# A long convolution and a soft mixture of experts: spectra stored and loaded in other shapes, x on other partitions, two loads moved within a step

## The chip, the cores and the metric

The kernel runs on one core of one Trainium2 chip, in float32 throughout. The metric is the device time of one execution in microseconds (us). Before the change it is 912.35 us, the median of three runs (912.24, 912.35 and 916.9 us).

## The reference

Two blocks follow each other. The first is a causal convolution of eight sequences of 5,696 steps and 128 channels with one filter as long as the sequence, by a Fourier transform:

```
Xf = np.fft.rfft(x, n=L, axis=1)        # L = 2 * 5696
Hf = np.fft.rfft(h, n=L, axis=0)
y  = np.fft.irfft(Xf * Hf[None], n=L, axis=1)[:, :S, :]
```

The second takes y as 45,568 tokens of 128 channels. With 8 experts of 4 slots each (32 slots), it mixes tokens into slots, runs the experts and mixes back:

```
logits = x @ phi                                  # (45568, 32)
d = softmax of logits over all tokens;  slot_input = d.T @ x
slot_out[e] = relu(slot_input[e] @ w1[e]) @ w2[e]
c = softmax of logits over the 32 slots;  out = c @ slot_out
```

## The kernel before

**The transform.** A sequence of 5,696 is taken as 89 rows of 64. The transform length is 5,760 = 90 x 64 (`N1`, `N2`). Its first stage runs over the rows and gives 90 frequencies k for each of the 64 columns n. Its second runs over the 64 columns for each k. `g` counts the transformed sequences: g = 0 is the filter `h`, g = 1 to 8 are the eight batches of x. A *chunk* is 4 columns and their 4 mirror columns (`CH = 4`), so a g has 8 chunks (`NJ`), and a *step* t of the main loop handles one chunk in the first stage. Steps 0 to 7 are the filter, 8 to 15 the first batch, and so on to step 71.

**Stage A** (`load_x`, `fold`, `stage_a`). `load_x` brings two chunks at once: 96 rows on partitions 0 to 95 (the filter: 89 rows), for each row 8 near columns and 8 far ones, 4 KB each. `fold` on GpSimd adds and subtracts near and far. `stage_a` multiplies by the table `s1`: its *low* part, each step, gives frequencies below `LOW` = 60 (64 columns of `s1`, 64 partitions for each of two parities `o`); its *high* part, each odd step, gives the other 30 for the two chunks of the last two steps, in four groups of 32 partitions. ScalarE evicts into the tile `fst` (four buffers), and the stores are put on a list `pending` that `flush()` issues later on SyncE's queue (SP). The spectra go to a DRAM tensor `f_g` of shape (90, 64, 2, 128): a low tile in two stores of 60 rows, a high tile in four stores of 30 rows, a row being 4 KB.

**Stage B** (`load_g`, `stage_b1`, `stage_b2`). A *unit* u is 8 frequencies of one g; a g has 12 units (the last has 2 frequencies). `load_g` loads a unit into `gt` (three buffers) as one transfer on 128 partitions, in packets of 1 KB. `stage_b1` does the 64-point transform on TensorE (`bt<-gt,wt`) and multiplies by the filter's spectrum on VectorE. One step later `stage_b2` transforms back (`bz<-yf,vt`), and ScalarE evicts to `zst`, which is stored to `zm` (the first 64 frequencies) or `zr` (the rest). Steps have one and two units in turn; the units of sequence g begin at step 9 + 8g. So unit 0 of a new g is used one step after that g's last chunk has been stored. `prefetch` loads units up to three ahead (`AHEAD = 3`), but those of g only from step 8(g + 1) on.

**Stage C** (`load_main`, `load_rest`, `stage_c1` to `stage_c6`). From step 27 on, each odd step takes a tile T of z, main part (`zc<-zm`) and rest (`zx<-zr`), finishes the inverse transform on TensorE (`bank<-zc,im` at L412, `bank<-zx,ir` at L417), and goes on to logits, softmax and dispatch. The z tiles of step t + 2 are loaded in odd steps; the rest of a batch's first tile, whose data has only just been stored, is loaded in the even step before it is used (t = 26, 34, ... 74).

**Order of the work.** The schedule is written out by hand: each engine executes its instructions in program order. Nearly all transfers are issued by SP in program order, so an SP issue that waits holds all later ones. In the compiled program the transfers carry eight completion counters in turn, and an issue waits until the transfer eight issues before it has landed; so at most eight are in flight.

An even step issues in this order: the first rest of a batch, if it is due; the load of x for step t + 4; the stores of the low spectra; then, around `stage_b1`, the next unit's spectra and the stores of z; then the softmax sums, the dispatch, and the second unit. The main loop ends at step 80, and a tail then finishes the last batch, the experts and the output (stores of `out_dram<-o`).

Of the kernel before, what the change touches and what calls it, by code (L numbers as in the profile page):

```python
# [18 lines left out]
def transform_tables(S, N1, N2, CH, LOW, MAIN, XR):  # L19

    N, R1, HALF, P = N1 * N2, S // N2, N2 // 2, 2 * N2
    k1 = np.arange(N1)  # L30
    alpha = np.pi * (k1 + 0.5) / N1
    m1 = np.arange(R1) - (N1 - 1) / 2
    a1 = np.outer(m1, alpha)
    part = np.stack([np.cos(a1), -np.sin(a1), -np.cos(a1)], 1)
    s1 = np.zeros((P, 2, 3, N2 + HALF))
    for i, r in enumerate((slice(0, R1), slice(XR - R1, XR))):
        s1[r, i, :, 0:LOW] = part[:, :, 0:LOW]
        s1[r, i, :, N2:N2 + N1 - LOW] = part[:, :, LOW:]
# [12 lines left out]
    a2 = m2[None, :, None] * omega[:, None, :]  # L51
    w = np.concatenate([np.cos(a2), np.sin(a2)], 1)
    back = np.arange(N2).reshape(2, HALF).T.reshape(-1)
    NU = (NP + 1) // 2
    turn = (N1 - 1) / 2 * alpha[:, None] + (N2 - 1) / 2 * omega
    wq = np.zeros((2, N2, NP, N2))
    vq = np.zeros((2, N2, NU, 2, N2))
    tn = np.zeros((2, N2, 2, (NU + 1) // 2, 2, 2))
    for a in range(2):
        wq[a] = w[a::2].transpose(1, 0, 2)  # L60
# [10 lines left out]
def kernel(  # L71
# [24 lines left out]
    nc = tc.nc  # L96
# [15 lines left out]
    HP = P // 2  # L112
    NQ = NJ // 2
    assert S == R1 * N2 and R1 == N1 - 1 and D == P and CH == Q == 4
    LOW, MAIN = 60, HP
    XR = -(-R1 // 16) * 16
    ctx.enter_context(tc.manual_schedule())

# [4 lines left out]
    fd = [nc.dram_tensor(f"f_{g}", (N1, N2, 2, D), F32, kind="Internal").ap() for g in range(B + 1)]  # L123
# [54 lines left out]
    def load_x(m, halves=((0, 2 * CH),)):  # L178

        if 2 * m >= (B + 1) * NJ:  # L180
            return
        g, j = divmod(2 * m, NJ)
        if g == 0:
            src, blocks = h, ((0, R1 // 16 * 16), (R1 // 16 * 16, R1))
        else:
            r0 = min((g - 1) * R1, B * R1 - XR) * N2
            src, blocks = x.rearrange("b t d -> (b t) d")[r0:r0 + XR * N2], ((0, XR),)
        src = src.rearrange("(a n) d -> a n d", n=N2)
        t_ = xcs[m % len(xcs)]
        for n0, n in halves:  # L190
            a = (CH * j + n0, N2 - CH * j - n0 - n)
            p = (n0, 2 * CH - n0 - n)
            for r0, r1 in blocks:
                if n == 2 * CH:
                    v = src[r0:r1, a[0]:a[0] + n, :]
                    v = bass.AP(tensor=v.tensor, offset=v.offset,
                                ap=[v.ap[0], [(a[1] - a[0]) * D, 2], [1, n * D]])
                    nc.sync.dma_start(
                        out=t_[r0:r1, :, :, :].rearrange("p s n d -> p s (n d)"), in_=v)
                    continue  # L200
                for s_ in range(2):
                    nc.sync.dma_start(
                        out=t_[r0:r1, s_, p[s_]:p[s_] + n, :].rearrange("p n d -> p (n d)"),
                        in_=src[r0:r1, a[s_]:a[s_] + n, :].rearrange("r n d -> r (n d)"))
        xs[2 * m] = xs[2 * m + 1] = t_

# [16 lines left out]
    def flush():  # L223
        while pending:
            pending.pop(0)()
# [4 lines left out]
    def stage_a(c, high):  # L230

        g, j = divmod(c, NJ)
        st = apool.tile([P, CH, 2, D], F32, name="fst", tag="fst", bufs=4)
        if high:
            groups = [(c_, o, HALF, slice(HP, HP + HALF)) for c_ in (c - 1, c) for o in range(2)]
# [28 lines left out]
    def load_g(u):  # L264
        if u >= (B + 1) * NW:
# [4 lines left out]
        nc.sync.dma_start(  # L270
            out=t_[:, 0:n, :, :].rearrange("p q c d -> p q (c d)"),
            in_=fd[g][8 * w:8 * w + 2 * n].rearrange("(q a) r c d -> (a r) q (c d)", a=2))
        gs[u] = t_

    def stage_b1(u):
# [355 lines left out]
    for t in range(last_front + 1):  # L631
# [58 lines left out]
                softmax_exp(U)  # L690
            flush()
        else:
            if pair(-1) is not None and pair(-1) % NQ == 0:
                load_rest(pair(-1))
            if t < NA:
                load_x(t // 2 + 2)
            flush()
            if t == NJ:
                prefetch(AHEAD - 1)
            slot_b()  # L700
            if W is not None:
                softmax_sum(W)
                dispatch(W)
# [229 lines left out]
```

## Time and profile before

| what | value |
|---|---|
| profiled execution, its own time | 909.23 us |
| its span in the profile | 907.4 us |
| median of the three timed runs | 912.35 us |
| TensorE (PE) busy | 760.2 us, 84% |
| VectorE (DVE) busy | 601.4 us, 66% |
| ScalarE (ACT) busy | 436.8 us, 48% |
| GpSimd (POOL) busy | 399.8 us, 44% |
| SP's transfer queue q1 | 275.74 MB, 89.7% of 16 transfer engines |
| all transfers | 278.33 MB, mean 307 GB/s |

The span is the time from the first to the last instruction that the profiler recorded. The busy shares are means over stages that differ: the filter and the first batches until about 200 us, the full pipeline from there to 640 us, the end of stages B and C to about 830 us, and the output. Which engine or queue ends the wait is read stage by stage. "DMA share" is the time that packets took, summed over the 16 transfer engines of the core and divided by 16 times the stretch; it can go slightly over 1. PEld is TensorE's loading of weights. SPq is SP's sequencer, and the length of one of its DMA entries is the time it took to issue, its own waiting in part included, not the time of the transfer.

### The profile page before, as it was taken

Reading aid. Unit: us, or ns where it says so; the run is one execution under the profiler, and the core shown is the slowest. Engines: PE = TensorE matmul, PEld = TensorE weight load, DVE = VectorE, ACT = ScalarE, POOL = GpSimd, SP = SyncE. Lnnn points to the kernel's source line nnn. Section 1 sums busy time; section 2 is a strip of 40 time slices with the busy share of each in tenths; the row PEclk is TensorE's granted clock in tenths of the full one; section 3 lists DMA queues with packets and bytes.
Section 4 is the critical chain, followed back from the end, with each engine's and each line's share of the span. In section 5 each row is a group of like instructions: output and inputs, shape, how many; then the busy total and the mean of one; then the engine's idle time right before and its main releaser. Section 6 shows DMA issues by size and latency. Waiting matters only on the chain.

```text
span 907.4 us, 21291 instructions
## 1 busy us (share of the span) xinstructions
PE 760.2 (84%) x8308; PEld 387.7 (43%) x8308; DVE 601.4 (66%) x896; ACT 436.8 (48%) x880; POOL 399.8 (44%) x353
## 2 busy tenths in 40 slices
PE   6857778689999989999998999799888877767893
PEld 2212233234444444444444444344444434344793
DVE  2029767568778867886877787678778766653552
ACT  2423234335556545665655655456544444563441
POOL 4634322444555655655655566456332224651000
PEclk9979889999999999999999999899988888766855
DMA  8989999999999999999999999999998768540798
GB/s 267 318 275 343 293 296 337 298 314 376 341 291 375 361 326 308 372 358 299 357 364 335 295 373 348 303 308 346 306 291 304 264 200 341 186 166 1 292 406 335
DMA packets 170443, 278.33 MB, mean 307 GB/s; under 512 B 13543, under 2 KB 128231, under 8 KB 165135
## 3 DMA queue, kind: packets, MB, share of 16 engines
q1 hardware_dynamic: 169336, 275.74, 89.7%
q10 hardware_dynamic: 1008, 1.25, 0.5%
q8 instruction: 66, 1.08, 0.5%
q14 instruction: 33, 0.27, 0.1%
HBM read 147.94 MB, written 129.00 MB: 305 GB/s over the span
## 4 chain that ended last, share of the span: by engine, by line
PE 47%; DMA 23%; ACT 8%; POOL 8%; DVE 6%; issue 6%; SPq 1%; ACTq 0%; DVEq 0%; POOLq 0%
PE bank L241 9%; DMA gt<-f 9%; PE bt L284 9%; PE bz L327 6%; POOL y L430 5%; PE bank L412 4%; DMA f<-fst 4%; PE op L886 3%; PE bank L439 3%; PE bank L417 3%; PE bank L448 2%; DMA zx<-zr 2%; ACT fst L243 2%; DMA out_dram<-o 2%; PE bank L527 2%
## 5 line engine op out<-in xcount | busy, mean ns | idle before, releaser
L241 PE MATMUL bank<-x,s 128*32 128x512 f32 (+1 forms) x1152 | 218.0, 620 | 12.9 <-POOL x L217 8.4
L217 POOL TENSOR_TENSOR x<-xc 128x512 f32<-128x512 f32 x144 | 180.4, 1278 | 107.2 <-PE bank L241 86.5
L284 PE MATMUL bt<-gt,wt 64*64 64x256 f32 x1620 | 125.0, 419 | 72.8 <-DMA gt<-f 33.0
L430 POOL TENSOR_TENSOR y<-y,op 128x512 f32<-128x512 f32 x64 | 77.6, 1213 | 206.8 <-DVE op L404 204.3
L304 DVE TENSOR_TENSOR pi<-bt,Hi 128x1024 f32<-128x1024 f32 x96 | 113.0, 1177 | 83.5 <-PE bt L284 83.3
L243 ACT ACTIVATE fst<-bank 128x512 f32<-128x512 f32 x216 | 122.8, 592 | 86.0 <-PE bank L241 57.7
L332 ACT ACTIVATE zst<-bz 128x1024 f32<-128x1024 f32 x96 | 93.3, 972 | 128.3 <-PE bz L327 109.4
L284 PEld LDWEIGHTS bt<-gt,wt 64*64 64x64 f32 x1620 | 58.3, 141 | 151.2 <-issue 79.1
L312 DVE TENSOR_TENSOR yf<-bt,pi 128x512 f32<-128x512 f32 x192 | 119.4, 663 | 3.3
L304 DVE TENSOR_TENSOR bt<-bt,Hr 128x1024 f32<-128x1024 f32 x96 | 113.0, 1177 | 0.0
L241 PEld LDWEIGHTS bank<-x,s 128*32 128x32 f32 (+1 forms) x1152 | 55.1, 126 | 129.8 <-issue 93.6
L327 PE MATMUL bz<-yf,vt 64*64 64x256 f32 x1440 | 110.4, 404 | 0.0
L327 PEld LDWEIGHTS bz<-yf,vt 64*64 64x64 f32 x1440 | 64.3, 143 | 25.5 <-issue 4.2
L512 POOL TENSOR_TENSOR L<-L,rs 128x512 f32<-128x512 f32 x32 | 33.5, 1048 | 91.6 <-DVE rs L511 66.4
L404 DVE TENSOR_TENSOR y<-bank,y 128x512 f32<-128x512 f32 x32 | 22.1, 692 | 76.7 <-ACT y L420 76.5
L439 PE MATMUL bank<-ident,y 109*128 109x109 f32 x512 | 62.7, 273 | 7.9 <-ACT yt L441 7.9
L504 ACT ACTIVATE L<-L 128x512 f32<-128x512 f32 x32 | 20.2, 630 | 94.7 <-POOL L L501 94.6
L430 POOL TENSOR_TENSOR y<-y,om 128x512 f32<-128x512 f32 x54 | 63.9, 1183 | 2.1
L439 PEld LDWEIGHTS bank<-ident,y 109*128 109x128 f32 x512 | 52.9, 149 | 19.4 <-POOL x L217 14.7
L412 PE MATMUL bank<-zc,im 64*64 64x512 f32 x480 | 60.8, 623 | 0.0
L441 ACT ACTIVATE yt<-bank 128x360 f32<-128x360 f32 x128 | 53.0, 482 | 7.7 <-PE bank L439 7.3
L420 ACT ACTIVATE y<-bank 128x512 f32<-128x512 f32 x32 | 19.1, 596 | 72.6 <-PE bank L417 72.6
(101 smaller groups left out, 862.5 us busy)
## 6 DMA issues: line engine op xcount, KB each, us to landing
gt<-f SPq DMA_DIRECT2D x99, 512.0 KB
f<-fst SPq DMA_DIRECT2D x144, 240.0 KB
zm<-zst SPq DMA_DIRECT2D x128, 256.0 KB
zc<-zm SPq DMA_DIRECT2D x30, 1024.0 KB
xc<-in_x_dram SPq DMA_DIRECT2D x32, 768.0 KB
f<-fst SPq DMA_DIRECT2D x144, 120.0 KB
out_dram<-o SPq DMA_DIRECT2D x16, 1024.0 KB
zx<-zr SPq DMA_DIRECT2D x30, 512.0 KB
```

The lines of the kernel that those rows point to most:

```text
L217: nc.gpsimd.tensor_tensor(out=y_[:, o, :, :], in0=near, in1=far, op=AL.subtract if o else AL.add)
L241: nc.tensor.matmul(p[i * m:(i + 1) * m, :], s1[:, g // B, q + o, cols], columns(c_, o), start=True, stop=True)
L243: nc.scalar.activation(st[:, :, q, :], p[:, :].rearrange("p (n d) -> p n d", d=D), AF.Copy)
L284: nc.tensor.matmul(bt[q * HP:(q + 1) * HP, a, o, :], wt[r, 2 * i + q, :], t_[r, 2 * o + q, :, :].rearrange("p c d -> p (c d)"), start=True ...
L304: nc.vector.tensor_tensor(out=p_, in0=pv, in1=h_, op=AL.mult)
L312: nc.vector.tensor_tensor(out=y_[r, 0:k, c, :], in0=pv[:, :, c, :], in1=pi[r, 0:k, 1 - c, :], op=op_)
L327: nc.tensor.matmul(bz[a * HP:(a + 1) * HP, q, o, :], vt[r, i, a, :], y_[r, a * m + o, :, :].rearrange("p c d -> p (c d)"), start=True, sto ...
L332: nc.scalar.activation(st[:, 0:m, 0:n, :].rearrange("p o q x -> p q o x"), bz[:, 0:n, 0:m, :], AF.Copy)
L412: nc.tensor.matmul(ps[o, c][h_ * HP:(h_ + 1) * HP, :], im[r, c, :], zt[r, h_, :, c, :], start=True, stop=False)
L430: eng.tensor_tensor(out=part_, in0=part(v, 0), in1=o_[:, :, :], op=sign)
L439: nc.tensor.transpose(p[:, i * TR:(i + 1) * TR], ys[T][0:TR, k * CH + i, 0:D], ident[0:TR, 0:TR])
L441: nc.scalar.activation(yt[:, k * CH:(k + 1) * CH, :, :], of_tokens(p), AF.Copy)
```

## The change

Four things change together.

- **Shape of the spectra.** `LOW` becomes 64. The low spectra of a g go to a tensor `fl_g` (parity, 64 frequencies, 32 columns, 2, 128), the high ones to `fh_g` (parity, chunk half, 32, 16 columns, 2, 128), of whose 32 rows 26 are used. Each `fst` tile is now stored whole, in one transfer of 128 rows of 4 KB. A unit of 8 frequencies now lies within one of the two tensors. It is loaded by two transfers (low, one for each parity, onto every second partition) or four (high, onto every fourth). The rows of the table `w` are put in the new order, and in the high part the four matmul groups change their order (parity outside, chunk inside).
- **x on every second partition.** Rows 0 to 63 go to partitions 1, 3, ... 127 and rows 64 to 95 to partitions 32, 34, ... 94, in two transfers in place of one (the filter's rows in three in place of two). The rows of `s1` move along.
- **A new g's first spectra** are loaded at the beginning of step 8(g + 1), ahead of the load of x and the flush, and no longer after that step's first `stage_b1`. There `prefetch` is called with the last unit still in the pipeline plus three, which loads unit 0 (for the filter, units 0 to 2).
- **z's first rest** is loaded after the load of x, after the flush, after the first slot of stage B and another flush.

```diff
-    for i, r in enumerate((slice(0, R1), slice(XR - R1, XR))):
+    spread = np.r_[1:P:2, N2 // 2:N2 // 2 + 2 * (XR - N2):2]
+    for i, r in enumerate((spread[0:R1], spread[XR - R1:])):
...
-    LOW, MAIN = 60, HP
+    LOW, MAIN = HP, HP
...
-    fd = [nc.dram_tensor(f"f_{g}", (N1, N2, 2, D), ...
+    fl = [nc.dram_tensor(f"fl_{g}", (2, LOW, HALF, 2, D), ...
+    fh = [nc.dram_tensor(f"fh_{g}", (2, 2, HALF, HALF // 2, 2, D), ...
...
-            src, blocks = x..., ((0, XR),)
+            src, edges = x..., (0, HP, XR)
...
-            for r0, r1 in blocks:
+            for r0, r1 in zip(edges, edges[1:]):
+                p0 = 2 * r0 - HP - HALF if r0 else 1
+                rows = slice(p0, p0 + 2 * (r1 - r0) - 1, 2)
...
-        k0, k1 = (LOW, N1) if high else (0, LOW)
-        for i, (c_, o, m, _) in enumerate(groups):
-            n0 = o * HALF + CH * (c_ % NJ)
-            pending.append(partial(
-                nc.sync.dma_start,
-                out=fd[g][k0:k1, n0:n0 + CH, :, :].rearrange("k n c d -> k (n c d)"),
-                in_=st[i * m:i * m + k1 - k0, :, :, :].rearrange("k n c d -> k (n c d)")))
+        if high:
+            dst, n0 = fh[g].rearrange("o h k m c d -> (o h k) m (c d)"), CH * (j // 2)
+        else:
+            dst, n0 = fl[g].rearrange("o k n c d -> (o k) n (c d)"), CH * j
+        pending.append(partial(
+            nc.sync.dma_start,
+            out=dst[:, n0:n0 + CH, :].rearrange("p n x -> p (n x)"),
+            in_=st[:, :, :, :].rearrange("p n c d -> p (n c d)")))
...
-        nc.sync.dma_start(
-            out=t_[:, 0:n, :, :].rearrange("p q c d -> p q (c d)"),
-            in_=fd[g][8 * w:8 * w + 2 * n].rearrange("(q a) r c d -> (a r) q (c d)", a=2))
+        if 8 * w < LOW:
+            src = [fl[g][o, 8 * w:8 * w + 2 * n] for o in range(2)]
+        else:
+            k0 = 8 * w - LOW
+            src = [fh[g][o, h_, k0:k0 + 2 * n] for o in range(2) for h_ in range(2)]
+        for i, v in enumerate(src):
+            nc.sync.dma_start(
+                out=t_[i::len(src), 0:n, :, :].rearrange("p q c d -> p q (c d)"),
+                in_=v.rearrange("(q a) r c d -> (a r) q (c d)", a=2))
...
-            if pair(-1) is not None and pair(-1) % NQ == 0:
-                load_rest(pair(-1))
+            if t % NJ == 0:
+                prefetch(wait_b2[-1] + AHEAD if wait_b2 else AHEAD - 1)
             if t < NA:
                 load_x(t // 2 + 2)
             flush()
-            if t == NJ:
-                prefetch(AHEAD - 1)
             slot_b()
+            if pair(-1) is not None and pair(-1) % NQ == 0:
+                flush()
+                load_rest(pair(-1))
```

More of the change, by code (lines that the diff above doesn't have):

```diff
@@ L52, in transform_tables @@
     w = np.concatenate([np.cos(a2), np.sin(a2)], 1)
+    near_low = np.arange(N2).reshape(2, HALF).T.reshape(-1)
+    near_high = np.arange(N2).reshape(2, -1, 2, CH).transpose(1, 3, 0, 2).reshape(-1)
     back = np.arange(N2).reshape(2, HALF).T.reshape(-1)
@@ L59, in transform_tables @@
     for a in range(2):
-        wq[a] = w[a::2].transpose(1, 0, 2)
+        for q in range(NP):
+            wq[a, :, q] = w[2 * q + a][near_low if 2 * q < LOW else near_high]
         for q in range(NP):
@@ L122 @@
                         transform_tables(S, N1, N2, CH, LOW, MAIN, XR))]
-    fd = [nc.dram_tensor(f"f_{g}", (N1, N2, 2, D), F32, kind="Internal").ap() for g in range(B + 1)]
+    fl = [nc.dram_tensor(f"fl_{g}", (2, LOW, HALF, 2, D), F32, kind="Internal").ap() for g in range(B + 1)]
+    fh = [nc.dram_tensor(f"fh_{g}", (2, 2, HALF, HALF // 2, 2, D), F32, kind="Internal").ap()
+          for g in range(B + 1)]
     zm = [nc.dram_tensor(f"zm_{b}", (2, MAIN, HALF, 2, D), F32, kind="Internal").ap() for b in range(B)]
@@ L183, in load_x @@
         if g == 0:
-            src, blocks = h, ((0, R1 // 16 * 16), (R1 // 16 * 16, R1))
+            src, edges = h, (0, HP, R1 // 16 * 16, R1)
         else:
             r0 = min((g - 1) * R1, B * R1 - XR) * N2
-            src, blocks = x.rearrange("b t d -> (b t) d")[r0:r0 + XR * N2], ((0, XR),)
+            src, edges = x.rearrange("b t d -> (b t) d")[r0:r0 + XR * N2], (0, HP, XR)
         src = src.rearrange("(a n) d -> a n d", n=N2)
@@ L198, in load_x @@
                     nc.sync.dma_start(
-                        out=t_[r0:r1, :, :, :].rearrange("p s n d -> p s (n d)"), in_=v)
+                        out=t_[rows, :, :, :].rearrange("p s n d -> p s (n d)"), in_=v)
                     continue
@@ L202, in load_x @@
                     nc.sync.dma_start(
-                        out=t_[r0:r1, s_, p[s_]:p[s_] + n, :].rearrange("p n d -> p (n d)"),
+                        out=t_[rows, s_, p[s_]:p[s_] + n, :].rearrange("p n d -> p (n d)"),
                         in_=src[r0:r1, a[s_]:a[s_] + n, :].rearrange("r n d -> r (n d)"))
@@ L234, in stage_a @@
         if high:
-            groups = [(c_, o, HALF, slice(HP, HP + HALF)) for c_ in (c - 1, c) for o in range(2)]
+            groups = [(c_, o, HALF, slice(HP, HP + HALF)) for o in range(2) for c_ in (c - 1, c)]
         else:
```

## The prediction

> **What bounds the kernel now.** I read the page first, then the busy times by stage, the rates of transfers in fine slices, TensorE's timeline for step lengths, and SP's timeline where a stall begins. The page has no engine that is full: PE 84%, SP's transfer queue 89.7%. By stage (columns: stretch, its length, then busy us and count of PE, PEld, DVE, ACT and POOL, PE's granted clock, DMA share, GB/s) it looks different:
>
> ```profile
> 20.00:50.00 30.00, 22.06 (x102) 6.42 (x98) 0.00 (x0) 11.07 (x20) 17.38 (x14) 0.94 0.96 310
> 57.00:105.00 48.00, 36.71 (x308) 12.40 (x305) 41.28 (x48) 14.33 (x24) 19.83 (x16) 0.93 0.96 309
> 105.00:165.00 60.00, 47.36 (x456) 20.39 (x456) 39.74 (x44) 23.18 (x32) 19.87 (x16) 0.88 0.93 292
> 206.00:640.00 434.00, 407.88 (x4672) 196.15 (x4670) 332.06 (x504) 248.76 (x505) 244.40 (x208) 0.98 1.00 338
> ```
>
> In the full pipeline (206 to 640) PE is busy 94% and the transfer engines 100%, at only 338 GB/s. The output stores at the end run at 406 GB/s. Why so slow in between? Slices of 0.25 us from 406 to 416 (the second line below), beside slices of 0.5 us of the output (the first):
>
> ```profile
> GB/s 418 401 406 410 414 401 406 406 414 406 406 393 414 434 373 385 406 406 406 410 406 410 406 406 401 414 406 406 401 414 410 406 406 406 434 377 393 389 414 410
> ...
> GB/s 371 340 373 332 354 340 279 328 148 131 180 131 246 262 311 262 295 246 262 246 229 217 311 414 397 385 360 311 401 401 365 442 348 340 350 356 356 344 340 348
> ```
>
> From 408 to 411.5 the rate falls to 131-311. SP's timeline (start, us, line, what, number) says what was queued there: x, then two f stores of 60 rows.
>
> ```profile
> 402.43 4.19 SPq L225 DMA_DIRECT2D f<-fst  x4
> 406.74 0.34 SPq L198 DMA_DIRECT2D xc<-in_x_dram  x1
> 407.17 0.88 SPq L225 DMA_DIRECT2D f<-fst  x2
> 408.14 2.52 SPq L270 DMA_DIRECT2D gt<-f  x2
> ```
>
> Behind them comes the new sequence's first unit, and PE waits for it. This happens once in each sequence; the timeline of PE (in brackets the idle time before, and the releaser):
>
> ```profile
> 250.88 1.09 PE L284 MATMUL bt<-gt,wt 64*64 64x256 f32 x16 [0.50 <-DMA gt<-f]
> ...
> 333.89 1.39 PE L284 MATMUL bt<-gt,wt 64*64 64x256 f32 x16 [3.36 <-DMA gt<-f]
> ...
> 416.39 1.95 PE L284 MATMUL bt<-gt,wt 64*64 64x256 f32 x16 [2.07 <-DMA gt<-f]
> ...
> 498.56 1.09 PE L284 MATMUL bt<-gt,wt 64*64 64x256 f32 x16 [1.69 <-DMA gt<-f]
> ...
> 583.22 1.99 PE L284 MATMUL bt<-gt,wt 64*64 64x256 f32 x16 [5.52 <-DMA gt<-f]
> ```
>
> Earlier there are the same waits, longer: 10.23 us at 56.80, 5.16 at 105.16, 3.11 at 172.03. Where no such wait falls, two steps take 20.15 us (low matmuls at 285.82 and 305.97), always the same, so that is compute. From step 29 on, eight steps take 79.78, 83.79, 82.55, 80.83 and 86.18 us (starts 206.04, 285.82, 369.61, 452.16, 532.99, 619.17). With the first one's own 0.50 taken off the floor is 79.3, so the boundary costs 16.7 us over the five sequences, the slow clock after each wait included (16 matmuls in 1.95 us for 1.09).
>
> **The change part by part.**
>
> *Stores of f and loads of x.* Each sequence has 12 f stores for 32, and 6.7% more f bytes (64 + 32 rows for 60 + 30). What a packet takes is in the trace's packet records: from 206 to 639 the 13,234 packets of 4,096 bytes (f, x, zx) have a median of 159 ns and a mean of 194, one in ten near 300, double; the 8,192-byte ones (zc) 309 and 367. All packets sum to 430 us of the 433. At their medians the two sizes would take 29 + 11 us less, and the extra rows 5 more: 395 us, a share of 0.91. Bounds: no relief (435 us with the extra rows) and full relief. I take full relief, because transfers of the new shapes are in this trace already: z's stores of 64 rows from every second partition are two fifths of the 1,024-byte packets, of which nine in ten take 46 ns or less, and the output's 128 rows run at 406 GB/s.
>
> In the pipeline this gives nothing by itself, since PE's 79.3 us per sequence hide it, but it shortens every queue. Where the queue is the bound it counts: in 20-50 the chain of waits is four landings of f in a row (18.91 for 9.80, 29.56 for 5.86, 35.85 for 7.51, 43.79 for 5.44). Packets there show about 5.5 us of excess in those 30, minus 1 for the rows: -4.5 (bounds 0 and -6; PE needs 22 of the 30).
>
> *The filter's loads* are 19 issues for 12, of which two come before the first fold. Eight took 3.71 us, so +0.9 there; the rest waits behind the tables in the queue or adds up to 3. I take +1.
>
> *The split unit loads.* 32 for 12 issues per sequence, and 8 for 4 of x: with f's 12 for 32 SP has 96 issues for 92, at 0.33 to 0.6 us each: +2 us of SP time in 79, hidden by SP's waiting for landings (the waits of SP's f and z issues for earlier transfers are over 100 us). 0; bounds 0 and +2 per sequence. The Trainium skill speaks against it: "DMA: Bandwidth & Descriptors", section "Rules for kernel authors", says two transfers to disjoint partition halves are not worth it and one of 128 partitions should be used, and "Anatomy of one DMA" gives a fixed 2.0 us for each (on another issue path). By that, 180 more unit loads would be up to 360 us one after another; the rows show up to eight in flight and 0.48 us per issue.
>
> *The first unit at the beginning of the step.* It no longer waits for x's issue and two f issues, and three of four high-f issues are gone: 402.43 + about 1 us for the one store is 403.4 for 408.14, 4.7 us earlier, and x (768 KB) and low f (480 KB) are no longer ahead in the queue, 3.7 us at 338 GB/s. Together 8 us earlier against a longest steady wait of 5.52, so these waits go. Of 16.7 us I take -15 (bounds -5 and -17). In exchange x is later by two issues and 512 KB, about 2.5 us; it is used three steps, 30 us, on. The load must find its low stores landed: they were issued in the middle of the step before, and in the pipeline 7 issues lie between.
>
> At the start fewer lie between, and SP stands until the last low store has landed. At 49.24 it did so already (the landing at 49.23 released it). Then the unit took 7.52 us with 1.25 MB ahead, which is 4 us at 310 GB/s: -4 (bounds -1 and -6). For 57-105, VectorE needs eleven filter units at 3.65 us (on the chain one begins at 64.95, the next at 68.64 and 72.23) and a short one of 1.9, 42 us; the first batch's unit came at 48.4, behind loads of 8.14, 6.88 and 7.12 us on the chain. Down to VectorE's floor, with the clock's 0.9: -5 (bounds -2 and -6). At 172.03: -3 (bounds 0 and -3.1). From 105 to 165 the waits of 2.99 us each pair are between PE and VectorE around one `bt` buffer: 0.
>
> *z's first rest.* Six times in the pipeline, and at step 26. It moves past x's two issues, the low store, the unit's loads and two z stores. SP now stands at the z stores until ScalarE's `zst` is done. At step 50: `zst` ends at 427.40, two z issues of 0.4-0.6 us, so zx is issued at about 428.5; before it was 430.01, because SP was late. PE reached L417 at 435.75 without waiting. From 428.5 there are 7.2 us, and when the step comes sooner, `zst` does too, so these 7.2 us stay. Landings of z on the chain took 4.9 to 6.5 us. So late by 0 to 1.5: +0.5 each, +3. At step 26, PE waited 2.28 us; zx goes from 185.22 to about 186.2 and more lies ahead: +1.5 (bounds 0 and +3). In return SP is no longer held by the landing of zr (5.68 us there on the chain). What queues behind the moved load are the step's later stores and the second unit, which is two steps ahead.
>
> *The high part's matmul order*: same count, same forms, 0. After 640: no wait for a unit shows, 0 (bounds -1 and +2).
>
> **The sum:** +1 - 4.5 - 4 - 5 - 3 + 1.5 - 15 + 3 = -26 us. The span 907.4 becomes 881.4, the profiled execution 909.23 becomes 883.2. The median is 3.1 us over that execution, so 912.35 - 26 gives 886. One measurement of this kernel can tell about 0.5% (4.6 us) from no change.
>
> **The rivals.**
>
> *Only the reorder works.* The conflicts between packets stay (x's 32 rows, f's 128). Then the share stays at 1.00 and queues stay long: 435 us of packets against 416 of steps at the floor. The stretch gains nothing beyond what the shorter way of the first unit buys early on: -4, -3 and -3, +4 for late zx, and -5 in the pipeline, about -11: 901. For: nothing here shows x's shape in 4 KB packets. Against: z's stores.
>
> *A wait for zx takes the gt waits' place.* If all eight places ahead hold 256 KB to 768 KB, up to 2.8 MB, a landing takes 8 us, as gt's 8.11: 1-3 us late, seven times, 7 to 21 us, the steady gain gone: between 895 and 910. The trace's four waits of PEld for zx sum to 5.9 us, so there is little slack.
>
> *The end on the other side: the split unit loads run into each other.* 64 or 32 rows per transfer put two transfer engines on the same partitions' ways. If their 1,024-byte packets doubled, as 4 KB ones do here, 30,000 packets at +46 ns over 16 engines are +86 us: 395 + 86 = 481 us for 433, +48, less 8 us of the start: about 952. It decides from +11 ns a packet (21 us, all the slack below 416), and the kernel is slower from about +30 ns. Against: the same shape stores at 46 ns.
>
> **How the numbers follow.** The sum 0.55, with its own range 874 to 895 from the bounds taken together; only the reorder 0.15; late zx 0.15; colliding loads 0.10; a start that loses more than its gain, with the rest near nothing, 0.05. Faster by over 0.5%: 0.55 + 0.14 + 0.09 = 0.78. Within: 0.07. Slower: 0.15, the collisions and part of the start. The range goes from 872, all upper gains, to 912, where the late zx has eaten all; the collisions are left out.
>
> **What would show it.** Right: the DMA share in the full pipeline falls to about 0.92 and no slice stays under 250 GB/s while x and f go; PE's waits for gt at the five boundaries are under 0.5 us and eight steps take 79-80 us; the first b1 comes at 48-50 us and the first batch's at 91-94. Wrong: PE's waits at L417 over 1.5 us each; 1 KB packets above 50 ns or a share of 1.00 with longer steps; SP standing at the first unit of a sequence for over 3 us.

## The result, and the profile after

The changed kernel takes 945.6 us (median of four runs, 943.0 to 946.6) where the kernel before takes 912.3 in the same comparison: 1.036 times as long, 95% interval 1.031 to 1.041. The forecast was 886, with a range that ended at 912. It went to the other side, in part by a rival that had been priced too low.

The busy times by stage of the changed kernel, columns as in the prediction (stretch, its length, busy us and count of PE, PEld, DVE, ACT and POOL, PE's granted clock, DMA share, GB/s):

```profile
8.00:20.00 12.00, 8.76 (x32) 2.25 (x32) 0.00 (x0) 4.76 (x7) 6.16 (x5) 1.00 0.82 249
20.00:50.00 30.00, 25.27 (x112) 7.72 (x112) 0.00 (x0) 12.17 (x22) 20.71 (x18) 0.94 0.99 370
57.00:105.00 48.00, 37.85 (x324) 12.90 (x316) 42.75 (x50) 14.76 (x25) 19.82 (x16) 0.96 0.94 317
206.00:640.00 434.00, 379.20 (x4296) 179.90 (x4294) 305.20 (x465) 228.01 (x464) 225.99 (x193) 0.96 0.94 318
```

The second line holds what was hoped of the wide transfers: 370 GB/s for 310. The last holds the loss. In the full pipeline PE is busy 379 us for 408, and the DMA share has indeed fallen from 1.00 to 0.94, but at 318 GB/s for 338: the transfer engines are not quicker, they now stand idle between transfers. Of the span's 37.2 us more (944.6 for 907.4), 4.6 lie before step 29 (it begins at 210.66 for 206.04), 33.2 in the next five times eight steps (446.3 us for 413.1), and -0.6 behind.

PE's waits for transfers, all in one view (the waits by instruction, operation and releaser: sum in us, count, longest):

```profile
PEld bank L432 <- DMA zx<-zr: 53.5, 7, 11.6
PE bank L432 <- DMA zx<-zr: 47.3, 6, 10.7
PE bt L299 <- DMA gt<-fl: 13.5, 6, 6.0
```

Before, PE had waited 33.0 us for `gt<-f` and 2.5 for zx; now it is 16.7 for gt (the line shown and 3.2 for `gt<-fh`) and 47.3 for zx. The two have changed places, and zx costs more than gt did. PE's timeline shows that it is z's first rest, once in each sequence:

```profile
279.04 1.81 PE L432 MATMUL bank<-zx,ir 26*64 26x512 f32 x16 [4.92 <-DMA zx<-zr]
367.13 2.01 PE L432 MATMUL bank<-zx,ir 26*64 26x512 f32 x16 [7.14 <-DMA zx<-zr]
459.23 2.01 PE L432 MATMUL bank<-zx,ir 26*64 26x512 f32 x16 [10.72 <-DMA zx<-zr]
548.76 2.02 PE L432 MATMUL bank<-zx,ir 26*64 26x512 f32 x16 [8.13 <-DMA zx<-zr]
638.77 2.02 PE L432 MATMUL bank<-zx,ir 26*64 26x512 f32 x16 [8.87 <-DMA zx<-zr]
```

The five waits sum to 39.8 us, against 13.1 us of gt waits in the same stretch before. After each wait the clock is slow for a while: the sixteen matmuls take 2.0 us, elsewhere 1.1, and in the 2.0 us from 459.23 on the granted clock is 0.50. SP's timeline in step 50 (start, us, line, what, number) and, below it, the chain of waits through the longest of them show how zx came to be late:

```profile
444.16 0.53 SPq L233 DMA_DIRECT2D fh<-fst  x1
446.58 1.16 SPq L206 DMA_DIRECT2D xc<-in_x_dram  x2
447.84 1.51 SPq L233 DMA_DIRECT2D fl<-fst  x1
449.45 1.61 SPq L285 DMA_DIRECT2D gt<-fl  x2
451.15 1.27 SPq L233 DMA_DIRECT2D zm<-zst  x2
452.47 0.65 SPq L400 DMA_DIRECT2D zx<-zr  x1
```

```profile
438.65 7.55 DMA zc<-zm
...
452.47 6.71 DMA zx<-zr
459.18 0.04 issue
459.23 2.01 PE bank L432 x16
```

First SP stands until 446.2 for the landing of an earlier zc, because x's issue needs the completion counter of the transfer eight issues before it. Then come seven issues, 5.9 us, and only then zx, which takes 6.7 us to land. Step 50 began at 435.01, so zx is issued 17.5 us into it. Before the change it was issued 7.5 to 9.9 us after the beginning of its step and landed 3.9 to 4.9 us later. In the pipeline that was just in time, between 0.2 us too late and 1.0 us early for PE's matmuls on it. The same step before, SP's timeline and PE's, where zx landed at 434.76:

```profile
430.01 0.35 SPq L385 DMA_DIRECT2D zx<-zr  x1
430.40 0.43 SPq L198 DMA_DIRECT2D xc<-in_x_dram  x1
```

```profile
435.75 1.11 PE L417 MATMUL bank<-zx,ir 26*64 26x512 f32 x16
```

### The profile page after: what moved, and what is told of

Its sections match the earlier page's. It is cut to its first block, busy times and chain, and to the rows that moved or that the text cites. A ratio compares the mean times of both kernels' runs of the same rounds, so it can differ in the third digit from the quotient of the medians.

```text
span 944.6 us, 21328 instructions
## 1 busy us (share of the span) xinstructions
PE 764.5 (81%) x8308; PEld 382.8 (41%) x8308; DVE 601.1 (64%) x896; ACT 437.0 (46%) x880; POOL 399.8 (42%) x353
## 3 DMA queue, kind: packets, MB, share of 16 engines
q10 hardware_dynamic: 1008, 1.25, 0.5%
## 4 chain that ended last, share of the span: by engine, by line
PE 48%; DMA 23%; ACT 8%; issue 6%; POOL 5%; SPq 4%; DVE 4%; DVEq 0%; ACTq 0%; POOLq 0%
PE bank L249 11%; PE bt L299 9%; PE bz L342 7%; DMA zx<-zr 5%; DMA out_dram<-o 4%; PE bank L427 4%; DMA zc<-zm 4%; PE bank L432 4%; PE bank L454 3%; POOL y L445 3%; PE bank L463 2%; ACT fst L251 2%; DMA fl<-fst 2%; ACT zst L347 2%; PE bank L542 2%
## 5 line engine op out<-in xcount | busy, mean ns | idle before, releaser
L249 PE MATMUL bank<-x,s 128*32 128x512 f32 (+1 forms) x1152 | 221.2, 621 | 14.8 <-POOL x L225 11.4
L432 PE MATMUL bank<-zx,ir 26*64 26x512 f32 x480 | 38.9, 707 | 47.3 <-DMA zx<-zr 47.3
L454 PEld LDWEIGHTS bank<-ident,y 109*128 109x128 f32 x512 | 52.5, 148 | 18.1 <-POOL x L225 13.3
```

The source lines that it names most:

```text
L432: nc.tensor.matmul(p[h_ * HP:(h_ + 1) * HP, :], ir[r, :], zx[r, h_, :, :], start=False, stop=True)
L454: nc.tensor.transpose(p[:, i * TR:(i + 1) * TR], ys[T][0:TR, k * CH + i, 0:D], ident[0:TR, 0:TR])
```

## The experiments

Five theories stood at the beginning. P (place): zx's new place alone costs the time. H (handed on): the earlier first unit gains nothing much, because zx becomes the wait. L: more transfers make SP late. Q: whole tiles put more bytes in flight and land later. C: split unit loads collide in the transfer engines. Unless said otherwise the edits stand against the kernel before.

**Each move and the shapes by themselves.** First the changed kernel with only z's first rest back in its old place:

```diff
         else:
+            if pair(-1) is not None and pair(-1) % NQ == 0:
+                load_rest(pair(-1))
             if t % NJ == 0:
...
             slot_b()
-            if pair(-1) is not None and pair(-1) % NQ == 0:
-                flush()
-                load_rest(pair(-1))
```

> The changed kernel with one part undone: z's first rest is loaded at the beginning of the step again, ahead of x. After the change PE stands 47.3 us at the rest's matmuls (six waits of 4.9 to 10.7 us). Theory P (place): zx is late because it was moved past seven issues that took 5.9 us (446.58 to 452.47). Then the six waits fall to under 20 us in sum and the time to 905-922. Theory L (late queue): zx is late because loads of units and x in pieces (40 issues of 0.6 us for 16 of 0.4-0.5 per sequence) make SP late everywhere. Then zx stays late: waits of 30 us or more, time 930 or more. Theory H (handed on): every boundary has one lateness of SP, which PE paid at the unit before and pays at zx once the unit is early; then what is left here is about what the units cost before, 2 to 5 us each, 10-20 us in sum, time 905-915, and part 4 alone shows the same.

926.6 us, 1.013 [1.009, 1.017]. The waits for zx fall from 47.3 to 13.5 us, as P has it, but those for gt rise from 16.7 to 25.3, and the time stays above P's range. The reverse edit, the kernel before with only this load moved:

```diff
-            if pair(-1) is not None and pair(-1) % NQ == 0:
-                load_rest(pair(-1))
             if t < NA:
                 load_x(t // 2 + 2)
             flush()
             slot_b()
+            if pair(-1) is not None and pair(-1) % NQ == 0:
+                flush()
+                load_rest(pair(-1))
```

> The kernel before with one part alone: z's first rest behind x, the stores, the unit's loads and another flush. P: zx goes out some 4 us later than now (430.0 to about 434 at step 50) and lands 5 us on, at 439 against a need at 435.75; 3-4 us late six or seven times, 20-25 us, time 930-937. L: without the pieces SP is not late; under 5 us, time 910-917. H: the unit still stands in the way and gives SP time; 0-10 us, 910-922.

942.8 us, 1.031 [1.026, 1.037]. Its waits, in the same view as above:

```profile
PE bank L417 <- DMA zx<-zr: 35.1, 6, 7.4
PE bt L284 <- DMA gt<-f: 17.6, 7, 9.2
```

P holds: one load moved by a slot, with nothing else changed, costs 28 us, a little more than P expected. In passing it takes nearly all waits for gt out of the pipeline (0.4 us left between 206 and 640), presumably because transfers catch up while PE stands for zx. A step that shows a wait vanish has not shown a gain.

Next the changed kernel with both moves undone, which leaves the shapes:

```diff
-            if t % NJ == 0:
-                prefetch(wait_b2[-1] + AHEAD if wait_b2 else AHEAD - 1)
+            if pair(-1) is not None and pair(-1) % NQ == 0:
+                load_rest(pair(-1))
...
             flush()
+            if t == NJ:
+                prefetch(AHEAD - 1)
             slot_b()
-            if pair(-1) is not None and pair(-1) % NQ == 0:
-                flush()
-                load_rest(pair(-1))
```

> The changed kernel with both moves undone: only the shapes of the spectra's transfers and x's partitions. P: no move, so zx is not late; the shorter queues shorten the units' waits; 895-908. L: zx is late by the pieces alone, 20 us or more of waits at the rest's matmuls, time 920 or more. H: units and zx share the lateness, sum of both waits in the pipeline near the 13 us of the units before, time 903-915.

931.2 us, 1.017 [1.014, 1.021]. The shapes too are a loss. The first-unit waits grow from 13.1 to 29.5 us in the pipeline, although 20 to 50 runs at 375 GB/s. The time is in L's range, but not by L's path: between 206 and 640 PE never waits for zx. Then the earlier first unit alone:

```diff
+            if t % NJ == 0:
+                prefetch(wait_b2[-1] + AHEAD if wait_b2 else AHEAD - 1)
             if t < NA:
                 load_x(t // 2 + 2)
             flush()
-            if t == NJ:
-                prefetch(AHEAD - 1)
             slot_b()
```

> The kernel before with one part alone: a new sequence's first spectra loaded at the beginning of the step. P and L: the units' five waits in the pipeline (13 us, 16.7 with what follows) shrink by more than half, nothing takes their place: 893-902. H: the units' waits go, and zx, which had 0 to 0.5 us to spare, is late by as much: waits at the rest's matmuls of 10 us or more in sum, time 905-915.

909.6 us, 0.993 [0.989, 0.997]: the only one of the four parts that pays, by 0.7%. Between 206 and 640 the waits for gt fall from 13.1 to 1.1 us as forecast, and 14.1 us of waits for zx appear where there were 0.2. H holds. The chain of waits through one of them shows why:

```profile
428.15 4.44 DMA zr<-zst
432.60 0.02 SPq L385
432.62 0.03 issue
432.65 5.12 DMA zx<-zr
437.77 0.04 issue
437.81 2.02 PE bank L417 x16
```

z's rest is a round trip through DRAM: stored, landed after 4.4 us, loaded, landed after 5.1. It starts from an eviction of the step before, so if PE no longer stands at the first unit it arrives earlier at L417, and the round trip is no shorter. Where the 0.7% is won the profile does not show: in this profiled execution, 913.8 us, the five times eight steps from step 29 take 420.5 us, no less than the 413.1 before.

**What in the shapes costs.** The unit loads split into as many pieces as in the change, with the old layout; x on every second partition alone, in two transfers; and the spectra's new shapes alone, with x and both moves as before:

```diff
-        nc.sync.dma_start(
-            out=t_[:, 0:n, :, :]..., in_=fd[g][8 * w:8 * w + 2 * n]...)
+        v = fd[g][8 * w:8 * w + 2 * n].rearrange("(q a) r c d -> (a r) q (c d)", a=2)
+        m = 2 if 8 * w < HP else 4
+        for i in range(m):
+            nc.sync.dma_start(out=t_[i::m, 0:n, :, :]..., in_=v[i::m])
```

> The kernel before, layout and order unchanged, with each unit loaded in two transfers on every second partition (units 0 to 7) or four on every fourth (units 8 to 11). Same bytes, same packets. The runs so far show the shapes alone at +16 us, with waits for the first unit of 5.3 to 6.9 us in the pipeline for 0.5 to 5.5 before. Theory L (late queue): an issue on alternate partitions takes SP 0.61 us where the whole one took 0.48, so 32 for 12 per sequence are 13.7 us more of SP's time; SP is late where it issues most, at the end of a sequence. Then the first units' waits grow by 3 us each and the time is 922-940. Theory Q (bytes in flight): eight transfers in flight are now whole tiles of 512 KB, so a load waits behind more bytes; the split by itself makes fewer bytes in flight and costs nothing: 905-917. Theory C (collisions): the split loads' 1,024-byte packets run into each other; their mean goes from 47 ns to 60 or more; 930 or more.

> The kernel before with x (and the filter) on every second partition, in two transfers (three for the filter) for one. L: 8 issues of 0.62 us for 4 of 0.38 per sequence, 3.5 us of SP's time: 0.5-1 us at each boundary, 0 to +8 us in all, 912-920. Relief (what the prediction counted on): x's packets no longer meet; the share of slow 4,096-byte packets falls from 0.17 to under 0.12 and the rate from 20 to 50 us from 310 to 330 GB/s or more: 902-910. If the slow packets of the pipeline are other transfers', the share stays above 0.15 there.

> The kernel before with the spectra's new shapes alone (whole stores, split unit loads), x in one transfer on partitions 0 to 95, both loads in their old places. L: SP's time per sequence is 13.7 more for the units and 6.9 less for the stores: a gain on the split alone, a little under the shapes with x: 918-928. Q: the whole stores are the cost, so 925-932, as with x, and above the split alone.

The split alone takes 979.1 us, 1.074 [1.067, 1.082]; x alone 929.7, 1.020 [1.014, 1.025]; the spectra alone 934.6, 1.025 [1.018, 1.031]. The first is above L's and Q's ranges, the other two are above every range that was set for them. C falls: in the split run's packet records the 1,024-byte packets take 48 ns in the mean, 47 before. Q falls as the only cause, since the split adds no byte and no whole tile and costs most. What the split adds is 20 transfers per sequence (112 for 92).

L then said that SP's own time for an issue was the cost. In the changed kernel's trace an issue onto every second partition or of a whole tile takes SP about 0.6 us (median of gt 0.61 for 0.48 before, f 0.54 for 0.42, x 0.62 for 0.38, some waiting included), which makes 10 us more per sequence. So in the run with z's rest back, the stores of f were given to ScalarE's queue:

```diff
-        pending.append(partial(
-            nc.sync.dma_start,
+        nc.scalar.dma_start(
             out=dst[:, n0:n0 + CH, :].rearrange("p n x -> p (n x)"),
-            in_=st[:, :, :, :].rearrange("p n c d -> p (n c d)")))
+            in_=st[:, :, :, :].rearrange("p n c d -> p (n c d)"))
```

> The changed kernel with z's first rest back at the beginning of the step (926 us), and the spectra's stores issued by ScalarE's queue right behind its own eviction, so SP has 84 issues per sequence for 96. Bytes, packets and shapes are the same. L: SP reaches the units and zx 3-6 us sooner at each boundary; their waits (25.0 and 13.5 us) halve; 903-918, unless ScalarE's own issues, 12 of 0.5 us per sequence, hold its evictions. Q: the same bytes are in flight; 922-930.

1008.1 us, 1.106 [1.099, 1.112]: an eighth of the issues less on SP, and 80 us worse, above every range. Over the whole run PE now waits 67 us for gt and 30 for zx; this was not taken apart further. L in this form fell. It left two readings: SP's time (L1), or the place that each transfer takes among the eight in flight (L2). Two runs took the count apart from the shape: 20 tiny extra loads per sequence, and the split onto whole halves and quarters of the partitions.

```diff
+        for i in range(1 if 8 * w < HP else 3):
+            s_ = bpool.tile([16, 32], F32, name="extra", tag="extra", bufs=12)
+            nc.sync.dma_start(out=s_[:, :], in_=h[0:16, 0:32])
```

> The kernel before, with 20 extra tiny loads per sequence (16 rows of 128 bytes, into scratch tiles that nothing reads), one beside each of the low units' loads and three beside each of the high ones: the number of transfers of the split unit loads, and none of their bytes or shapes. If the count costs (each transfer takes one of the eight places in flight, so SP is later with everything behind): as much as the split loads alone, 965 to 980. If only SP's issue time costs (20 x 0.35 to 0.45 us, 7 to 9 us per sequence of about 80): 925 to 950. If it is the shape of the split loads (half the partitions per transfer): 910 to 918.

```diff
+        m = P // (2 if 8 * w < HP else 4)
+        for i in range(0, P, m):
+            nc.sync.dma_start(out=t_[i:i + m, 0:n, :, :]..., in_=v[i:i + m])
```

> The kernel before, with the unit loads split into two and four transfers as in the split alone (979.1), but onto whole halves and quarters of the partitions and not onto every second or fourth. If the count of transfers costs: the same, 970 to 985. If SP's issue time costs and rows on every second partition are what makes an issue take 0.6 us: issues of 0.4 to 0.5 us and 945 to 965. If the landing of spread rows were the cause: 915 to 930.

994.3 us, 1.086 [1.080, 1.092], for 180 loads of 2 KB each that nothing reads; and 1008.7 us, 1.101 [1.094, 1.108], for whole halves; both are above the range that the count was given, by 14 and 24 us. Rows on every second or fourth partition are not the cost, for whole halves cost more (why they cost some 25 us more was not settled), and transfers without any bytes to speak of cost as much: at a ratio of 1.086 the 180 loads cost 79 us, 0.44 us each, though they move 0.37 MB in all. PE's waits with the tiny loads:

```profile
PE bt L287 <- DMA gt<-f: 79.9, 18, 10.5
PE bank L415 <- DMA zc<-zm: 18.1, 7, 3.5
```

Then the same tiny loads on other queues, first ScalarE's, then GpSimd's (`nc.scalar` and `nc.gpsimd` for `nc.sync`):

> The kernel before with the 20 tiny loads per sequence of the run of tiny extras (994.3), issued by ScalarE's queue and not by SP's. L1 (SP's own time for the issue is what costs): SP has as many issues as before, ScalarE gets 20 x 0.05 to 0.5 us per sequence of 80, 55% of which it is idle: 912 to 925. L2 (a transfer takes one of the eight places, and the next issues wait for it): as with SP's, 970 to 1000, since both queues share the eight.

> The same tiny loads issued by GpSimd's queue. Both L1 and L2 expect 912 to 920 if GpSimd's issues neither use SP's time nor its eight places. If they cost GpSimd about 1 us each, 20 us per sequence beside the 45 of 80 that it is busy: up to 930. As much as 970 or over would refute both, and leave something that every transfer costs, wherever it comes from.

1042.4 us, 1.139 [1.133, 1.146], on ScalarE's queue, and 922.0 us, 1.008 [1.005, 1.012], on GpSimd's. In the traces the landings of ScalarE's tiny loads count on the same eight semaphores as those of SP's transfers (100 and 102 to 108), GpSimd's on eight others (111 to 118). ScalarE's go through a transfer queue of their own (q10: 6,768 packets for 1,008 before), so a place in SP's transfer queue is not what they take. PE's and ScalarE's waits with ScalarE's queue:

```profile
PE bt L287 <- DMA gt<-f: 101.4, 24, 13.6
PE bank L415 <- DMA zc<-zm: 30.0, 11, 4.1
ACT zst L335 <- DMA extra<-in_h_dram: 21.3, 12, 2.8
```

and with GpSimd's:

```profile
PE bt L287 <- DMA gt<-f: 25.4, 9, 9.6
PEld bank L420 <- DMA zx<-zr: 5.3, 5, 2.0
```

Between 206 and 640 PE's waits for transfers are 13.3 us before, 52.6 with the tiny loads on SP, 64.0 on ScalarE and 5.0 on GpSimd; the slower the kernel, the fewer of its steps this stretch holds. L1 as the whole cause falls: with ScalarE, SP issues no more than before. L2 holds for these loads: what costs is a place among the eight, taken in order. On ScalarE it costs more, and more than the 970 to 1000 of L2, because the engine that stands for a place is the one that has to evict (21.3 us in front of `zst`).

**Does that hold for the change itself?** The changed kernel with z's rest back, and its extra pieces on GpSimd's queue (72 transfers per sequence left on SP for 96); and the same with x's eight transfers there instead (88 left):

```diff
-            nc.sync.dma_start(
+            (nc.gpsimd if i else nc.sync).dma_start(
                 out=t_[i::len(src), 0:n, :, :].rearrange("p q c d -> p q (c d)"),
```

> The changed kernel with z's first rest back at the beginning of the step (926.6), and the second to fourth pieces of the unit loads and the second of x issued by GpSimd's queue: 72 transfers per sequence on SP for 96, and 24 on GpSimd at 0.5 to 0.6 us each. If the places in flight are what the shapes cost: waits for gt and zx fall to under 10 us together and the time to 895 to 910, below the kernel with only the unit moved (909.6). If GpSimd stands for a buffer of a unit (free only when TensorE has used it) or for stores to land, its folds come late: 930 to 1000. If the places are not it: 920 to 930.

> The changed kernel with z's first rest back at the beginning of the step (926.6), and all eight transfers of x per sequence issued by GpSimd's queue: 88 on SP for 96. If a place is worth 0.45 us: 8 x 0.45 x 8 = 29 us less, 897 to 908. In the kernel with the old shapes four places less bought nothing (911.0 beside 909.6), by which this is 918 to 927. If x landing later delays the folds: over 930.

919.0 us, 1.007 [1.003, 1.010], and 930.6 us, 1.020 [1.011, 1.029], beside 926.6 with all on SP. With the pieces moved, PE's waits for transfers between 206 and 640 fall from 26.3 to 4.7 us, the least of all runs, so the places were what the pieces cost. The time follows in part: the five times eight steps from step 29 take 84.7 us each in the mean, for 87.9 with all on SP, but 82.6 before, so 895 to 910 was not reached. PE now waits 5.0 us for GpSimd's folds, which it never did in that stretch before, and GpSimd has 24 issues of 0.54 to 0.66 us per sequence more. The same is seen with the tiny loads on GpSimd (84.2 us per eight steps, 4.2 us of waits for folds). These means are of one profiled execution each; for the earlier unit alone, whose median is below the kernel before, it is 84.1, so 2 us are near what one execution can tell. That PE waits for the folds is seen; that this is all of the remaining 2 us was not tried. x's eight places were worth nothing, against the expectation: 22.3 us of waits remain.

The number of transfers per sequence is also not all of it. The spectra alone have 92, as many as before, and cost 23 us. So where in the step a transfer comes, or how long it keeps its place, counts too; no run separates these.

**How far the load may move, and whether the unit's gain can be kept.** z's first rest moved past x and the flush only, and not past the slot of stage B:

```diff
-            if pair(-1) is not None and pair(-1) % NQ == 0:
-                load_rest(pair(-1))
             if t < NA:
                 load_x(t // 2 + 2)
             flush()
+            if pair(-1) is not None and pair(-1) % NQ == 0:
+                load_rest(pair(-1))
             slot_b()
```

> The kernel before, with z's first rest moved past x's load and the flush of the two low stores only, and not past the first slot of stage B: a smaller dose of the move that alone gave 942.8. If the wait is SP's delay alone: three issues, 1.3 to 1.6 us, with a slack near zero before, so +1.5 us and the slow clock behind it at six places: 920 to 928, waits for zx of 1 to 3 us each. If what counts is the bytes that x and f put ahead (1.25 MB, 3.7 us at 338 GB/s): waits of 4 to 6 us, 932 to 942. If z's stores, which SP stands for in the slot, were the whole of it: 910 to 916.

925.2 us, 1.012 [1.008, 1.016], with waits for zx of 2.9 to 4.9 us: 11 of the 28 us, for three of the issues. Three further runs start from the earlier unit (909.6): high stores held back, in two places, and x on GpSimd's queue.

```diff
-            flush()
+            while len(pending) > (4 if t % NJ == NJ - 1 and t < NA else 0):
+                pending.pop(0)()
```

> The kernel before with the first unit at the beginning of the step (909.6 alone), and the four high stores of a sequence's last chunk held back from the end of the odd step until behind x in the next one, so that z's first rest has 480 KB less ahead of it (1.4 us at 338 GB/s) and four issues fewer (up to 2 us, if z's stores have landed by then). If the gain of the earlier unit is lost to zx for want of 1 to 3 us: waits for zx fall from 18.8 to under 8 us and the time is 896 to 903. If SP's later issues (the low units, the stores) take it over again: 905 to 912.

> The kernel before with the first unit at the beginning of its step (909.6 alone), and the four high stores of the odd step just ahead of z's first rest held back until behind this rest and x: 480 KB less ahead of the rest (1.4 us at 338 GB/s), and its issue up to 2 us earlier, not before z's stores have landed. Waits for zx fall from 18.8 to under 8 us, and the time to 896 to 904. If the landing of z's stores sets the issue anyway: only the 1.4 us at six places, 900 to 908. If the held stores come in the way of the next loads: 908 to 918.

> The kernel before with the first unit at the beginning of its step (909.6 alone), and x's loads (4 per sequence of 92 transfers) issued by GpSimd's queue. If each transfer less on SP's queue is worth 0.45 us, as the tiny extras cost: 4 x 0.45 x 8 = 14 us, 892 to 900, bounded by the floor of 79.3 us for eight steps. If GpSimd's issue delays its folds by a microsecond or more, or x then lands later than it is folded: 905 to 925.

The first hold was put in the wrong step: `t % NJ == NJ - 1` is the step before the first unit, three steps ahead of z's rest, so the rest had as much ahead of it as ever. It gave 917.3 us, 1.003 [1.000, 1.006], and more waits for zx (24.7 us in all for 18.8). With the hold in the right step (`t % NJ == 1`) it is 925.2 us, 1.010 [1.004, 1.017], above every range. The chain of waits of this run:

```profile
435.77 4.77 DMA zr<-zst
440.54 0.02 SPq L385
440.56 0.03 issue
440.59 4.36 DMA zx<-zr
```

The rest does land 0.8 us sooner behind its issue here (4.36 for 5.12; 0.4 in the mean of six steps), but its issue stands for the landing of z's stores, whatever is queued between, and the held stores now come behind it in one piece of six. x on GpSimd's queue is 911.0 us, 0.993 [0.989, 0.998], the same as without it. The best version found is the kernel before with its first unit earlier, 0.7% faster with x on either queue.

## Why the prediction was wrong, point by point

- **z's first rest, "late by 0 to 1.5: +0.5 each, +3".** This is the step that failed, and the largest. The working let zx go out at 428.5, behind two z stores, and took SP to be there in time. It counted the issues that the load moves past by name and then did not add them up: x's two, the low store, the unit's two, z's two, 5.9 us in the trace, behind an SP that itself stood for a counter. Measured alone, the move costs 28 us and not 3; on top of the rest of the change it costs 19 (945.6 for 926.6). Alone, the moved rest, the shapes and the earlier unit come to +28, +16 and -6, together 38 us, near the 33 measured. The rival "zx takes the gt waits' place" was the right mechanism with a wrong price: 1 to 3 us at a time, where PE waited 4.9 to 10.7.
- **The first unit, -15.** The waits for gt went, as forecast (13.1 to 1.1 us between 206 and 640). The time came back only by half of that: alone it is -0.7%, some 6 us over the whole kernel, its start included. The step left out asked "what is late next" of x only, which is 30 us early, and not of zx, whose round trip through DRAM had at most 1.0 us of slack in the pipeline before. In the changed kernel the gt waits are gone in part because PE stands at zx: with z's rest back in its old place they are 13.2 us between 206 and 640 again.
- **The split unit loads, "0, hidden by SP's waiting".** Wrong in kind. SP's long waits for landings were read as idle time into which issues fit (and the issues take 10 us more per sequence, not 2). They were the sign that the places were taken, so a further transfer adds a wait. The split alone costs 68 us (the ratio times 912), 0.38 us for each of 180 further loads. With the new layout and f's 20 fewer stores per sequence it is 23 us (the spectra alone, 92 transfers as before), so these pay most of it back, and all shapes together end at +16. The prediction weighed the page "DMA: Bandwidth & Descriptors" of the Trainium skill, whose "Rules for kernel authors" prefer one transfer of 128 partitions to two of disjoint halves, and set it aside; the split runs agree with the rule. The 2.0 us that the prediction took from "Anatomy of one DMA" are the fixed time of one transfer on another path; one more transfer cost 0.38 to 0.51 us here, since up to eight overlap.
- **The colliding loads (952).** This rival came nearest the measured time, and for the wrong reason: 1,024-byte packets take 48 ns.
- **Packet relief, a share of 0.91 at 395 us.** It came at the start (310 to 370 GB/s) and not in the pipeline: 4,096-byte packets average 190 ns there for 194, and the lower share is idle time. Stores of z and the output were the wrong rows to take it from; why it stays away when loads and stores are mixed was not settled.
- **The start, +1 - 4.5 - 4 - 5 - 3, a gain of 15.5.** By step 26 the kernel is 4.3 us ahead (171.00 for 175.33), by step 29 it is 4.6 behind. Between lies the wait for zx in step 26 (7.57 for 2.28, where +1.5 was forecast). So the start won 4.3 us and lost 8.9 around the moved rest; with z's rest back, step 29 begins at 199.03, 7.0 us earlier than before. The 20-to-50 rate was right. The filter's loads in more pieces cost more than +1. They are 21 issues for 14, not 19 for 12; the first twelve take 8.22 us where eight took 3.71, the first matmul comes at 10.32 us for 8.36 (x alone: 10.27), and 8 to 20 runs at 249 GB/s for 346. The first unit comes at 54.86 (48 to 50 forecast, 56.80 before) and the first batch's at 102.37 (91 to 94 forecast, 105.16 before), with 57 to 105 at 317 GB/s for 309. That the pieces of the filter's units take places there as in the pipeline is argued, not shown.
- **Right:** the high part's matmul order cost nothing (stage A's matmuls take 621 ns in the mean for 620), nothing happened at the end (-0.6 us behind step 69), and the gt waits of the pipeline vanished in the kernel with the earlier unit alone.

Open is why x on every second partition costs 2% alone. The cost lies in the pipeline (five times eight steps take 432.6 us for 413.1) and in the waits for the first units there (27.8 us for 13.1). It brings four more transfers per sequence, and eight of x fewer on SP brought nothing.

## What to carry to other kernels

When a load is moved within a queue that issues in order, add up every issue it moves past, with the waits they stand in, and compare with the slack in the rows of before; a landing just in time has none, and every wait that the change removes elsewhere makes it late. A queue that keeps standing for earlier landings has no free time for more issues: here one more transfer of 2 KB cost 0.44 us, so do not split transfers there without a reason. And ask of each vanished wait which load's round trip ends next.

## What the runs showed of the hardware that was not expected

- 180 loads of 2 KB cost 79 us on SP's queue, 127 on ScalarE's and 7.5 on GpSimd's (ratios 1.086, 1.139 and 1.008 of 912 us). The page "DMA: Bandwidth & Descriptors" of the Trainium skill says under "Rules for kernel authors" that spreading transfers over SP, ACT and GpSimd saves only sequencer time. Here the issuing engine decided, by the completion counters that it shares.
- An issue of the same load takes SP longer when it goes to every second or fourth partition, though it moves less: x 0.63 us for 0.34 (median of x alone, and of the split alone, where x is whole; 206 to 640). For unit loads the median mixes waits in (0.62 also with the rest moved alone, where they are whole); the lower quartile is 0.60 us in the split alone, 0.44 on whole halves and quarters and 0.39 before.
- In the new shapes (the changed kernel, and the shapes without the moves) the transfers run at 370 and 375 GB/s from 20 to 50 us, where loads of x and stores of spectra are nearly alone, for 310 before; in the full pipeline at 318 and 325, for 338 before.
